# State update ahead of the state read, and the first chunk in order of arrival, in an mLSTM cell followed by a GELU MLP

## The chip, the core and the metric

The kernel runs on one core of a Trainium2 chip. The metric is the time of one execution in microseconds of the device. The engines have short names in all that follows: PE is TensorE (PEld is its weight load), DVE is VectorE, ACT is ScalarE, POOL is GpSimd, and SP is SyncE, which here only issues transfers. Names with a q behind them (ACTq, SPq) are an engine's own queue, where transfers are issued.

## What is computed

The first half is a recurrence over 768 steps for 4 batches of 8 heads of 40 values, and the second half is an MLP of the exact GELU over its output, seen as 3072 tokens of 320 values. The weights arrive as 64-bit floats.

```
for t in range(S):
    m_new = max(f[t] + m, i[t])
    C = exp(f[t] + m - m_new) * C + exp(i[t] - m_new) * outer(v[t], k[t])
    n = exp(f[t] + m - m_new) * n + exp(i[t] - m_new) * k[t]
    m = m_new
    y[t] = sigmoid(o[t]) * (C @ q[t]) / max(abs(n @ q[t]), 1)
x = y as (4 * 768, 320)
out = gelu(x @ w_in) @ w_out          # w_in 320 x 2048, w_out 2048 x 320
```

## The kernel before

The sequence is cut into 6 chunks of 128 steps. Within a chunk the recurrence becomes an attention: the scores of a batch (`scores`, L281: products of turned keys and queries, tile `ps`) are multiplied by weights `W` that hold the gates, and `values` (L323) sums the values with them. What comes from earlier chunks is a second term: the state of the batch (`state`, one tile per batch) is read by the queries (L303), scaled by `gT` into `far` (L306) and added in `values` (L332). The state is then updated for the next chunk: POOL scales the old one by `dec` (L320), PE makes the chunk's own part from keys and weighted values `vw` (L311), and DVE adds the two (L321). Read and update share one tile of PSUM, `pf`: its first 8 columns of heads are the read, the last 4, named `pc`, are the update.

The gates come first. DVE scans `f_gate` to `bl`, subtracts it from `i_gate` to `a`, and a running maximum of `a` gives `M`, chunk by chunk (L147 to L159). `M` goes out to DRAM (`M_d`, L155 for the first chunk and L161 for the rest, both issued by ACT) and comes back copied to all 128 partitions, one tile `Mb` of 512 KB for each batch of each chunk (`load_M`, L113; the first three are issued by ACT, the rest by SP). POOL masks it (L254) and ACT makes `W` from it by 8 exponentials (L257, `weights_of`). Two further gate tiles, `ew` and `gg`, get an exponential (L166, L167), are turned by PE (L172) and copied to `ewT` and `gT`; `dec` is a product of `gT` (L175).

Of the first chunk's steps `turn` (L271) turns keys and queries of a batch on PE and ACT copies them out as `kT` and `qT` (L279); `output_gate` is the sigmoid of `o_gate` (L262); `values` ends in `hs` (copied by ACT in chunk 0, L334), which DVE and POOL divide and gate to `y` (L338 to L345); `turn_y` (L349) turns `y` on PE, and DVE and ACT copy it to `xT` (L356, L357), which the MLP reads.

The weights come as pairs of 32-bit words, in 10 pieces of `w_in` and 16 of `w_out` (`fetch`, L199; four buffers). `convert(i)` (L210) does on DVE and ACT the first half of piece i (L219 to L226; its `pow` goes through ACT twice, L221 and L222) and the second half of piece i - 1 (L231, L233), and then fetches piece i + 3. Ten pieces of `w_in` feed the up projection: its first four steps need pieces 0 to 4, its last four need pieces 5 to 9.

The order is written out by hand: each engine runs its instructions in the order in which the code emits them. A chunk's `run` (L359) emits the steps of four batches, and between them `fill`: in chunk 0 that is `convert`, in later chunks it is groups of four matmuls of the down projection (`po`, L403) of the chunk before. Then comes the up projection (`pu`, L388, and the GELU on ACT, L391). In chunk 0 the remaining conversions and the loads of the next six batches stand between the up steps (L426 to L433). Every batch's q, k, v and o_gate are four transfers of 160 KB by SP (`load`, L96). A chunk's `weights_of(n)` also asks for `Mb` of batch n + NM, where NM is the number of `Mb` buffers.

Of the kernel before, what the change touches and what calls it, by code (L numbers as in the profile page):

```python
# [9 lines left out]
F32 = mybir.dt.float32  # L10
# [10 lines left out]
def kernel(  # L21
# [32 lines left out]
    NM = 3  # L54
    NB = 4
    WP = 512
    assert S % L == 0 and DFF % (4 * WP) == 0 and DM % R == 0 and DM <= WP and D <= DP and NLD > B == 4
# [36 lines left out]
    M_d = dram.tile([BH, S], F32, name="M_d")  # L94
# [36 lines left out]
    for t in state:  # L131
# [15 lines left out]
    nc.vector.tensor_tensor_scan(out=bl.rearrange("p c l -> p (c l)"), data0=keep.rearrange("p c l -> p (c l)"),  # L147
                                 data1=f_sb.rearrange("p c l -> p (c l)"), initial=0.0, op0=OP.mult, op1=OP.add)
    nc.vector.tensor_tensor(out=a, in0=i_sb, in1=bl, op=OP.subtract)
    for c in range(NCH):  # L150
        nc.vector.tensor_tensor_scan(out=M[:, c], data0=a[:, c], data1=a[:, c], initial=m0[:, c:c + 1],
                                     op0=OP.max, op1=OP.max)
        if c == 0:

            nc.scalar.dma_start(out=M_d[:, 0:L], in_=M[:, 0])  # L155
            for n in range(NM):
                load_M(n, nc.scalar)
        if c + 1 < NCH:
            nc.vector.tensor_tensor(out=m0[:, c + 1:c + 2], in0=bl[:, c, L - 1:L], in1=M[:, c, L - 1:L], op=OP.add)  # L159

    nc.scalar.dma_start(out=M_d[:, L:S], in_=M[:, 1:NCH].rearrange("p c l -> p (c l)"))  # L161
# [3 lines left out]
                            in1=M[:, 1:NCH], op=OP.subtract)  # L165
    nc.scalar.activation(out=ew, in_=ew, func=AF.Exp)  # L166
    nc.scalar.activation(out=gg, in_=gg, func=AF.Exp)  # L167
    for src, dst in ((a, aT), (ew, ewT), (gg, gT)):
        n = dst.shape[1]
        pg = ps_tr.tile([P, n, BH], F32, name="pg", tag="tr")  # L170
        for c in range(n):
            nc.tensor.transpose(pg[:, c, :], src[:, c, :], ident[0:BH, 0:BH])  # L172
        nc.vector.tensor_copy(out=dst, in_=pg)
    pd = ps_tr.tile([P, NCH - 1, BH], F32, name="pd", tag="tr")
# [293 lines left out]
```

## Time and profile before

| | |
|---|---|
| Median of 3 runs | 627.89 us (627.11 to 629.42) |
| The profiled execution | 629.21 us, its span 627.3 us |
| PE busy | 554.4 us (88%) in 3850 matmuls |
| PEld busy | 358.1 us (57%) |
| ACT busy | 230.1 us (37%) in 516 |
| DVE busy | 199.0 us (32%) in 442 |
| POOL busy | 81.3 us (13%) in 130 |
| Granted clock of PE, mean | 0.961 |
| Moved by DMA | 43.62 MB in 136233 packets |

The profiled execution is 1.3 us above the median. Busy shares are averages over stages that differ: PE is busy nearly all the time from the first up projection on, and much less in the first 70 us. So the table says only where to look: at PE's own waits, and at the first chunk.

### The profile page before, as it was taken

The page shows a single profiled execution, that of the slowest core. Times are in us where ns is not written, and L with a number is a line of the kernel's source. Part 1 is how long each engine was busy: PE and PEld are TensorE (multiplying, and loading weights), DVE is VectorE, ACT ScalarE, POOL GpSimd, SP SyncE. Part 2 cuts the span into 40 slices and gives each one's busy share as a digit, 9 for nine tenths or more (in the row PEclk, how much of TensorE's full clock was granted, in tenths as well). Part 3 has the DMA queues.
Part 4 walks back from the last instruction along what each step waited for, and adds up shares of the span by engine and source line. Part 5 has one row for each costly group of instructions (what it writes and reads, how often), then busy time and mean ns, then how long its engine had stood idle before and what let it go on. Part 6 is the DMA issues. An engine that isn't in the chain of part 4 may idle for free.

```text
span 627.3 us, 9450 instructions
## 1 busy us (share of the span) xinstructions
PE 554.4 (88%) x3850; PEld 358.1 (57%) x3850; DVE 199.0 (32%) x442; ACT 230.1 (37%) x516; POOL 81.3 (13%) x130
## 2 busy tenths in 40 slices
PE   0637698778999998899999899999899999999997
PEld 0536354456764466764476664476664477754575
DVE  5457686834630013630013630013630014500000
ACT  0775274683022283022284022284022293122200
POOL 4212300012230011230011230011220001100000
PEclk9967699889999999999999999999999999999999
DMA  9999199735430034530034530035200010000000
GB/s 161 208 211 184 37 161 207 178 104 103 76 64 0 1 112 90 82 64 2 0 108 92 81 67 1 0 101 96 46 22 0 1 44 13 11 11 0 1 21 21
DMA packets 136233, 43.62 MB, mean 70 GB/s; under 512 B 101248, under 2 KB 134048, under 8 KB 136192
## 3 DMA queue, kind: packets, MB, share of 16 engines
q1 hardware_dynamic: 132976, 41.36, 33.3%
q10 hardware_dynamic: 3216, 1.67, 1.0%
q8 instruction: 30, 0.49, 0.4%
q14 instruction: 11, 0.09, 0.1%
HBM read 38.99 MB, written 4.03 MB: 69 GB/s over the span
## 4 chain that ended last, share of the span: by engine, by line
PE 49%; issue 38%; POOL 6%; DMA 3%; SPq 2%; DVE 1%; POOLq 0%; ACTq 0%; ACT 0%; DVEq 0%
PE po L403 25%; PE pu L388 11%; PE ph L329 3%; PE ps L293 3%; POOL state L320 2%; POOL Mb L254 2%; DMA Mb<-M_d 2%; PE pf L303 2%; PE pf L311 2%; PE pt L276 2%; SPq L102 2%; PE px L355 1%; SPq L208 1%; POOL vw L286 1%; DMA M_d<-M 1%
## 5 line engine op out<-in xcount | busy, mean ns | idle before, releaser
L403 PE MATMUL po<-w_out,g 128*128 128x320 f32 x768 | 221.0, 437 | 0.0
L388 PE MATMUL pu<-xT,w_in 64*128 64x512 f32 x960 | 215.5, 604 | 3.2 <-ACT g L391 2.8
L403 PEld LDWEIGHTS po<-w_out,g 128*128 128x128 f32 x768 | 141.2, 191 | 52.6 <-issue 1.2
L388 PEld LDWEIGHTS pu<-xT,w_in 64*128 64x128 f32 x960 | 100.6, 192 | 115.7 <-issue 109.5
L296 DVE TENSOR_TENSOR W<-ps,W 128x512 f32<-128x512 f32 x48 | 30.9, 685 | 259.0 <-PE ps L293 259.0
L391 ACT ACTIVATE g<-pu 128x512 f32<-128x512 f32 x96 | 52.0, 593 | 131.9 <-PE pu L388 131.9
L357 ACT COPY xT<-px 64x384 f32<-64x384 f32 (+1 forms) x48 | 17.9, 420 | 128.3 <-DVE xT L356 128.3
L257 ACT ACTIVATE W<-Mb,aT 128x128 f32<-128x128 f32 x192 | 58.1, 393 | 1.8 <-POOL Mb L254 1.7
L320 POOL TENSOR_TENSOR state<-state,dec 64x164 f32<-64x164 f32 x32 | 14.8, 462 | 286.2 <-PE pf L303 285.0
L311 PE MATMUL pf<-vw,kb 128*64 128x41 f32 x320 | 14.1, 239 | 32.1 <-POOL state L320 19.5
L254 POOL TENSOR_SCALAR_AFFINE_SELECT Mb<-Mb 128x1024 f32<-128x1024 f32 x24 | 27.0, 1145 | 80.2 <-DMA Mb<-M_d 80.0
L406 ACT COPY o_sb<-po 128x320 f32<-128x320 f32 x24 | 10.2, 426 | 61.5 <-PE po L403 40.7
L311 PEld LDWEIGHTS pf<-vw,kb 128*64 128x64 f32 x320 | 12.2, 146 | 35.0 <-POOL state L320 21.7
L338 POOL TENSOR_TENSOR y<-hs,ob 128x320 f32<-128x320 f32 x24 | 19.4, 809 | 97.8 <-DVE hs L332 72.1
L293 PEld LDWEIGHTS ps<-qT,kT 64*128 64x128 f32 x384 | 25.8, 205 | 10.1 <-issue 10.1
L293 PE MATMUL ps<-qT,kT 64*128 64x128 f32 x384 | 30.4, 302 | 0.0
L329 PE MATMUL ph<-vb,W 128*64 128x41 f32 x768 | 28.6, 236 | 0.0
L329 PEld LDWEIGHTS ph<-vb,W 128*64 128x64 f32 x768 | 26.4, 145 | 2.4 <-issue 2.2
L356 DVE COPY xT<-px 64x384 f32<-64x384 f32 (+1 forms) x48 | 21.1, 476 | 17.5 <-PE px L355 16.7
L276 PE MATMUL pt<-ident,kb 128*128 128x128 f32 x96 | 17.2, 308 | 9.3 <-ACT kT L279 9.3
L279 ACT COPY kT<-pt 128x512 f32<-128x512 f32 x24 | 14.0, 584 | 30.8 <-PE pt L276 30.6
L355 PE MATMUL px<-ident,y 128*128 128x128 f32 x120 | 18.4, 287 | 6.8 <-ACT xT L357 6.0
(71 smaller groups left out, 352.9 us busy)
## 6 DMA issues: line engine op xcount, KB each, us to landing
Mb<-M_d SPq DMA_DIRECT2D x21, 512.0 KB, 4.0
bits<-in_moe_w_in_dram SPq DMA_DIRECT2D x20, 256.0 KB, 5.6
bits<-in_moe_w_out_dram SPq DMA_DIRECT2D x16, 320.0 KB, 4.2
qb<-in_q_dram SPq DMA_DIRECT2D x24, 160.0 KB, 4.4
kb<-in_k_dram SPq DMA_DIRECT2D x24, 160.0 KB, 4.8
vb<-in_v_dram SPq DMA_DIRECT2D x24, 160.0 KB, 4.3
ob<-in_o_gate_dram SPq DMA_DIRECT2D x24, 160.0 KB, 3.9
out_dram<-o_sb SPq DMA_DIRECT2D x24, 160.0 KB, 1.8
```

Of the source, the lines that this page charges most:

```text
L254: nc.gpsimd.affine_select(out=M_n, in_=M_n, compare_op=OP.is_ge, fill=1.0e30, base=0, pattern=[[0, H], [1, L]], channel_multiplier=-1)
L257: nc.scalar.activation(out=W[n][:, h, :], in_=M_n[:, h, :], func=AF.Exp, scale=-1.0, bias=aT[:, c, b * H + h:b * H + h + 1])
L276: nc.tensor.transpose(pt[:, p, :], src[n % NLD][:, 2 * p:2 * p + 2, :].rearrange("p h d -> p (h d)"), ident)
L293: nc.tensor.matmul(ps[hip][:, p, :], kT[r, p, :], qT[r, p, :], start=True, stop=True)
L296: nc.vector.tensor_tensor(out=w, in0=ps[hip], in1=w, op=OP.mult)
L311: nc.tensor.matmul(pc[halves[hip], p, :], kb[n % NLD][:, 2 * p + hip, :], vw[:, 2 * p + hip, :], start=True, stop=True)
L320: nc.gpsimd.tensor_tensor(out=st, in0=st, in1=d.to_broadcast([DP, NP, D1]), op=OP.mult)
L329: nc.tensor.matmul(ph[r, h, :], Pm[:, h, r], vb[n % NLD][:, h, :], start=True, stop=True)
L355: nc.tensor.transpose(px[:, k, :], ys[:, (k0 + k) * R:(k0 + k + 2) * R], ident)
L388: nc.tensor.matmul(pu[e], w_in[r, k, f // 2 * P:(f // 2 + 1) * P], xT[r, (k - e) % NK, :], start=(k == 0), stop=(k == NK - 1))
L391: nc.scalar.activation(out=g[:, f + e, :], in_=pu[e], func=AF.Gelu)
L403: nc.tensor.matmul(po, g[:, f, b * L:(b + 1) * L], w_out[:, f, :], start=(f == 0), stop=(f == NF - 1))
```

## The change

It has three parts, and each keeps what is computed.

1. In `scores` the eight pairs of matmuls that make `pc` stand ahead of the state read, not behind it and `far`.
2. The first chunk has an order of its own, `run_first`. The first chunk's part of `bl`, `a` and `M` is made ahead of the other five chunks' part. All four `Mb` tiles of chunk 0 are issued by ACT at once (NM is 4). The rest of `M` goes out through SP's queue, behind the first four pieces, and no longer through ACT's. The turning of `a` is followed by `turn(0)`, and that of `ew` and `gg` comes behind it (`decays`). Each batch then goes through `turn`, `scores`, `turn_y` of the batch before, `output_gate`, `values` and one `convert`.
3. `M_d` is stored by chunk, so that a batch's row of `Mb` is one line of 4 KB and not eight of 512 bytes; a transfer of a `w_in` piece has 64 lines of 4 KB and not 256 of 1 KB. `w_in` then holds other columns side by side, and the up step pairs blocks f and f + 4.

```diff
-    NM = 3
+    NM = 4
...
-    M_d = dram.tile([BH, S], F32, name="M_d")
+    M_d = dram.tile([NCH, BH, L], F32, name="M_d")
...
-        eng.dma_start(out=Mb[n], in_=M_d[b * H:(b + 1) * H, c * L:(c + 1) * L]
-                      .unsqueeze(0).to_broadcast([P, H, L]))
+        eng.dma_start(out=Mb[n].rearrange("p h l -> p (h l)"),
+                      in_=M_d[c, b * H:(b + 1) * H, :].rearrange("h l -> (h l)").unsqueeze(0).to_broadcast([P, H * L]))
...
+    for c0, c1 in ((0, 1), (1, NCH)):
+        flat = lambda t: t[:, c0:c1].rearrange("p c l -> p (c l)")
+        nc.vector.tensor_tensor_scan(out=flat(bl), data0=flat(keep), data1=flat(f_sb), initial=0.0,
+                                     op0=OP.mult, op1=OP.add)
+        nc.vector.tensor_tensor(out=a[:, c0:c1], in0=i_sb[:, c0:c1], in1=bl[:, c0:c1], op=OP.subtract)
+        for c in range(c0, c1):
+            nc.vector.tensor_tensor_scan(out=M[:, c], data0=a[:, c], data1=a[:, c], initial=m0[:, c:c + 1],
+                                         op0=OP.max, op1=OP.max)
...
+        if c0 == 0:
+            nc.scalar.dma_start(out=M_d[0], in_=M[:, 0])
+            for n in range(B):
                 load_M(n, nc.scalar)
...
-    nc.scalar.dma_start(out=M_d[:, L:S], in_=M[:, 1:NCH].rearrange("p c l -> p (c l)"))
...
-            src = src.rearrange("k (m two x) -> k m two x", two=2, x=2 * P)
-            pieces.append(([(slice(R * e, R * e + R), src[:, :, e, :]) for e in range(2)],
-                           w_in[:, blk, f0 // 2:f0 // 2 + WP]))
+            pieces.append(([src[:, 2 * WP * e:2 * WP * (e + 1)] for e in range(2)], w_in[:, blk, f0 // 2:f0 // 2 + WP]))
...
+    fetch(0)
+    load(1)
+    fetch(1)
+    load(2)
+    fetch(2)
+    load(3)
+    fetch(3)
+    nc.sync.dma_start(out=M_d[1:NCH].rearrange("c p l -> p c l"), in_=M[:, 1:NCH])
...
             pc = pf[:, H:H + NP, :]
+            if c + 1 < NCH:
+                for p in range(NP):
+                    for hip in range(2):
+                        nc.tensor.matmul(pc[halves[hip], p, :], kb[n % NLD][:, 2 * p + hip, :], vw[:, 2 * p + hip, :],
+                                         start=True, stop=True)
             if c > 0:
...
             if c + 1 < NCH:
-                for p in range(NP):
-                    for hip in range(2):
-                        nc.tensor.matmul(pc[halves[hip], p, :], kb[n % NLD][:, 2 * p + hip, :], vw[:, 2 * p + hip, :],
-                                         start=True, stop=True)
...
+        def run_first(self):
+            self.turn(0), weights_of(0), convert(0)
+            decays()
+            self.scores(0), weights_of(1), convert(1)
+            self.turn(1), weights_of(2), weights_of(3), output_gate(0), self.values(0), convert(2)
+            self.scores(1), self.turn_y(0), output_gate(1), self.values(1), convert(3)
+            self.turn(2), self.scores(2), self.turn_y(1), output_gate(2), self.values(2), convert(4)
+            self.turn(3), self.scores(3), self.turn_y(2), output_gate(3), self.values(3), convert(5)
+            self.turn_y(3)
...
-    conv = feeder([lambda i=i: convert(i) for i in range(len(pieces) + 1)])
-    first = feeder([lambda: conv(1)] * (n_in // 2 + 1))
-    Cell(0).run(first)
+    Cell(0).run_first()
+    conv = feeder([lambda i=i: convert(i) for i in range(n_in // 2 + 1, len(pieces) + 1)])
```

Two places of the order are needed below. The first is PE in the first batch of chunk 1, between the down projection's matmuls; `ps` are the scores, `pf` from `state` is the state read, `pf` from `vw` is the update. Before:

```order
L403 MATMUL po<-w_out,g 128x320 [waits DVE_49] x4
L293 MATMUL ps<-qT,kT 128x128 x8
L303 MATMUL pf<-state_97,qT 64x82 x8
L311 MATMUL pf<-vw,kb_111 64x41 [waits DVE_49,Pool_49]
L311 MATMUL pf<-vw,kb_111 64x41 x7
L403 MATMUL po<-w_out,g 128x320 x4
```

With the change:

```order
L424 MATMUL po<-w_out,g 128x320 [waits DVE_49] x4
L301 MATMUL ps<-qT,kT 128x128 x8
L311 MATMUL pf<-vw,kb_111 64x41 [waits Pool_49]
L311 MATMUL pf<-vw,kb_111 64x41 x7
L316 MATMUL pf<-state_97,qT 64x82 x8
L424 MATMUL po<-w_out,g 128x320 [waits DVE_49] x4
```

The update went ahead of the read and lost its wait for DVE; the read behind it waits for nothing. Its wait for POOL stands for `vw`.

The second place is ACT in chunk 0, from the `hs` of one batch to the `hs` of the next. Before:

```order
L334 COPY hs<-ph 128x328
L221 ACTIVATE pow<-pow,e_hi 128x512
L222 ACTIVATE pow<-pow,e_lo 128x512
L279 COPY kT<-pt 128x512
L279 COPY qT<-pt 128x512
L317 COPY state_99<-pf 64x4x41 x2
L334 COPY hs<-ph 128x328
```

With the change:

```order
L343 COPY hs<-ph 128x328
L225 ACTIVATE pow<-pow,e_hi 128x512
L226 ACTIVATE pow<-pow,e_lo 128x512
L287 COPY kT<-pt 128x512
L287 COPY qT<-pt 128x512
L326 COPY state_99<-pf 64x4x41 x2
L366 COPY xT<-px 64x3x128
L366 COPY xT<-px 64x2x128
L270 ACTIVATE ob_121<-ob_121 128x320
L343 COPY hs<-ph 128x328
```

Before, `hs` of a batch stood behind the turning of the batch two further on, and only one conversion stood in that stretch of the chunk. With the change, `hs` of a batch stands behind a conversion, its own batch's turning, and the copies of the batch before.

## Rows read from the trace of the kernel before

**Rows 1.** The waits of PE: line, for whom, us in total, times, longest

```profile
PE pf L311 <- POOL state L320: 19.5, 16, 1.2
PE pf L311 <- POOL vw L286: 12.6, 2, 10.5
```

**Rows 2.** The timeline in chunk 1, second batch: start, us, engine, line, [idle before <-releaser]

```profile
141.69 1.16 PE L293 MATMUL ps<-qT,kT 64*128 64x128 f32 x16
142.78 0.79 PE L303 MATMUL pf<-state,qT 128*64 128x82 f32 x16
142.95 1.29 DVE L296 TENSOR_TENSOR W<-ps,W 128x512 f32<-128x512 f32 x2 [5.79 <-PE ps L293]
143.66 1.00 POOL L320 TENSOR_TENSOR state<-state,dec 64x164 f32<-64x164 f32 x2 [5.80 <-PE pf L303]
144.16 0.49 DVE L306 TENSOR_TENSOR far<-pf,gT 128x328 f32<-128x328 f32 x1
144.79 0.67 PE L311 MATMUL pf<-vw,kb 128*64 128x41 f32 x16 [1.22 <-POOL state L320]
145.25 1.14 PE L329 MATMUL ph<-vb,W 128*64 128x41 f32 x32
```

**Rows 3.** The timeline of the first 26 us: gates, M and the first weights

```profile
3.06 1.75 DVE L147 TENSOR_TENSOR_SCAN bl<-keep,f_sb 32x768 f32<-32x768 f32 x1 [1.22 <-DMA f_sb<-in_f_gate_dram]
...
5.82 0.47 DVE L151 TENSOR_TENSOR_SCAN M<-a,m 32x128 f32<-32x128 f32 x1
...
11.02 2.98 ACTq L113 DMA_DIRECT2D Mb<-M_d  x3
...
16.15 1.28 ACT L166 ACT_TABLE_LOAD   x1 [16.15 <-DMA Mb<-M_d]
...
16.36 1.09 POOL L254 TENSOR_SCALAR_AFFINE_SELECT Mb<-Mb 128x1024 f32<-128x1024 f32 x1 [9.36 <-DMA Mb<-M_d]
...
18.09 0.72 ACT L167 ACTIVATE gg<-gg 32x640 f32<-32x640 f32 x1
...
23.20 2.45 ACT L257 ACTIVATE W<-Mb,aT 128x128 f32<-128x128 f32 x8
```

**Rows 4.** The timeline from the first `hs` of chunk 0 to the first up matmul

```profile
46.13 1.55 ACT L262 ACTIVATE ob<-ob 128x320 f32<-128x320 f32 x4
...
49.56 0.43 ACT L334 COPY hs<-ph 128x328 f32<-128x328 f32 x1
...
52.11 1.56 PE L329 MATMUL ph<-vb,W 128*64 128x41 f32 x32
...
52.51 0.72 ACT L221 ACTIVATE pow<-pow,e_hi 128x512 f32<-128x512 uint32 x1 [2.52 <-DVE pow L219]
...
54.36 0.59 ACT L279 COPY qT<-pt 128x512 f32<-128x512 f32 x1
...
54.79 1.28 DVE L296 TENSOR_TENSOR W<-ps,W 128x512 f32<-128x512 f32 x2
...
55.77 2.08 PE L293 MATMUL ps<-qT,kT 64*128 64x128 f32 x16
...
58.01 0.87 DVE L356 COPY xT<-px 64x384 f32<-64x384 f32 x2
...
58.58 0.75 ACT L357 COPY xT<-px 64x384 f32<-64x384 f32 x2 [2.69 <-DVE xT L356]
...
70.14 1.99 PE L388 MATMUL pu<-xT,w_in 64*128 64x512 f32 x2 [0.22 <-DVE xT L356]
```

**Rows 5.** Windows: stretch, its us, busy of PE, PEld, DVE, ACT, POOL, PEclk, DMA, GB/s

```profile
50.00:58.00 8.00, 5.53 (x73) 4.83 (x75) 7.49 (x17) 3.31 (x7) 3.05 (x4) 0.66 0.94 200
62.70:72.00 9.30, 3.96 (x14) 2.61 (x16) 6.95 (x15) 3.79 (x8) 4.89 (x5) 0.69 0.02 4
```

**Rows 6.** The line that issues `Mb` (L113), first 40 us, six transfers

```profile
DMA to landing us min/median/max: 5.3/7.3/11.4
```

**Rows 7.** The timeline where chunk 1 starts, PE

```profile
127.90 1.11 PE L276 MATMUL pt<-ident,kb 128*128 128x128 f32 x4 [6.97 <-ACT kT L279]
```

More of the change, by code (lines that the diff above doesn't have):

```diff
@@ L146 @@
     nc.vector.memset(m0[:, 0:1], -1.0e30)
[L147 to L156, printed above, removed]
+    for c0, c1 in ((0, 1), (1, NCH)):
[7 more added lines that the diff above has]
+            if c + 1 < NCH:
+                nc.vector.tensor_tensor(out=m0[:, c + 1:c + 2], in0=bl[:, c, L - 1:L], in1=M[:, c, L - 1:L],
+                                        op=OP.add)
+        if c0 == 0:
+            nc.scalar.dma_start(out=M_d[0], in_=M[:, 0])
+            for n in range(B):
                 load_M(n, nc.scalar)
[L158 to L161 removed]
     nc.vector.tensor_tensor(out=ew, in0=a[:, 0:NCH - 1],
@@ L165, with gates_turned, decays @@
                             in1=M[:, 1:NCH], op=OP.subtract)
+    def gates_turned(parts):
+        for src, dst in parts:
+            n = dst.shape[1]
+            pg = ps_tr.tile([P, n, BH], F32, name="pg", tag="tr")
+            for c in range(n):
+                nc.tensor.transpose(pg[:, c, :], src[:, c, :], ident[0:BH, 0:BH])
+            nc.vector.tensor_copy(out=dst, in_=pg)
+    gates_turned([(a, aT)])
     nc.scalar.activation(out=ew, in_=ew, func=AF.Exp)
     nc.scalar.activation(out=gg, in_=gg, func=AF.Exp)
[L168 to L174, printed above, removed]
-    nc.tensor.matmul(pd.rearrange("p c n -> p (c n)"), last, gT.rearrange("p c n -> p (c n)"), start=True, stop=True)
-    nc.vector.tensor_copy(out=dec, in_=pd)
-    gate_ctx.close()
-    gp = ctx.enter_context(tc.tile_pool(name="gp", bufs=1))
+    def decays():
+        gates_turned([(ew, ewT), (gg, gT)])
+        pd = ps_tr.tile([P, NCH - 1, BH], F32, name="pd", tag="tr")
+        nc.tensor.matmul(pd.rearrange("p c n -> p (c n)"), last, gT.rearrange("p c n -> p (c n)"),
+                         start=True, stop=True)
+        nc.vector.tensor_copy(out=dec, in_=pd)
     w_src = {}
@@ L201, in fetch @@
             return
-        parts, dst = pieces[i]
+        src, dst = pieces[i]
         bits[i] = raw.tile([P, WP, 2], U32, name="bits", tag="bits", bufs=NB)[:, 0:dst.shape[1], :]
-        for r, src in parts:
-            to = bits[i][r].rearrange("p n two -> p (n two)")
-            if len(src.shape) == 3:
-                to = to.rearrange("p (m x) -> p m x", x=2 * P)
-            nc.sync.dma_start(out=to, in_=src)
+        to = bits[i].rearrange("p n two -> p (n two)")
+        for e in range(len(src)):
+            nc.sync.dma_start(out=to[P // len(src) * e:P // len(src) * (e + 1)], in_=src[e])
     def convert(i):
@@ L235, in convert @@
             fetch(i + NB)
-    for n in range(B):
-        if n > 0:
-            load(n)
-        fetch(n)
+    fetch(0)
[6 more added lines that the diff above has]
+    nc.sync.dma_start(out=M_d[1:NCH].rearrange("c p l -> p c l"), in_=M[:, 1:NCH])
     halves = (slice(0, R), slice(R, P))
@@ L380, in up_steps, with step @@
     def up_steps(g):
-        def step(f):
+        def step(i):
+            f = i // (WP // P) * 2 * (WP // P) + i % (WP // P)
             pu = [ps_mm.tile([P, TG], F32, name="pu", tag="mm") for e in range(2)]
-            for k in range(NK):
+            for blk in range(NK):
                 for e in range(2):
                     r = halves[e]
-                    nc.tensor.matmul(pu[e], w_in[r, k, f // 2 * P:(f // 2 + 1) * P], xT[r, (k - e) % NK, :],
-                                     start=(k == 0), stop=(k == NK - 1))
+                    nc.tensor.matmul(pu[e], w_in[r, blk, i * P:(i + 1) * P], xT[r, (blk - e) % NK, :],
+                                     start=(blk == 0), stop=(blk == NK - 1))
             for e in range(2):
-                nc.scalar.activation(out=g[:, f + e, :], in_=pu[e], func=AF.Gelu)
-        return [lambda f=f: step(f) for f in range(0, NF, 2)]
+                nc.scalar.activation(out=g[:, f + e * (WP // P), :], in_=pu[e], func=AF.Gelu)
+        return [lambda i=i: step(i) for i in range(NF // 2)]
     def down_steps(c, g):
```

8 lines of the change are left out of this document (6 added, 2 removed).

## The prediction

> **What bounds the kernel now.** I read the waits of PE first, since PE is busy nearly throughout after the first 70 us. Two of them matter for this change. PE waits 16 times for 1.2 us ahead of the state update, 19.5 us in all [rows 1]: once for each of 4 batches in each of chunks 1 to 4 (chunk 0 has no state to read, chunk 5 none to update). And in chunk 0 it waits for `vw`, 10.5 us the longest time [rows 1]. Next I read the timeline of one of the 16 waits [rows 2]. The state read ends about 143.57. PE then stands until 144.79. In that time POOL scales the old state (143.66 to 144.66), and DVE, which is busy with the weights until 144.24, makes `far` (144.16 to 144.65). The view puts the wait down to POOL, which ended last; the built order names DVE as well. Nothing else of PE's is held there: the update needs only `vw` and keys, and the matmuls behind it, `ph`, start as soon as it is through. Every stage after 133 us is of this kind, PE's own work in a row with this one hole, so 1.22 us saved there is 1.22 us of the end.
>
> Last I read the timeline of chunk 0, which ends with the first up matmul at 70.14 [rows 4]. Here no engine is full. DMA is, until about 60 us (0.94 busy in 50 to 58, and 0.02 in 62.7 to 72 [rows 5]); then a chain over ACT, DVE, POOL and PE runs out, batch by batch.
>
> **Part 1, the update ahead of the read.** No instruction is added or removed: 16 matmuls of 0.67 us and 16 of 0.79 change places [rows 2]. The update then waits for `vw` alone. PE's waits for `vw` are two in the whole run, and the long one lies in chunk 0 [rows 1], so in chunks 1 to 4 `vw` is early even for a place 2 us further ahead (0.8 us of read and 1.2 of wait). The read waits for nothing, as its state was finished a chunk ago. So the hole closes: 16 x 1.22 = **19.5 us**. What comes later instead: POOL's scaling and `far` start when the read ends, now 0.67 us later against the scores but 1.2 us or so earlier against the end; DVE has its weights until then anyway (142.95 to 144.24 [rows 2]). The state is next read a chunk later. Nothing waits for `hs` sooner than the turning of `y`, which stands behind the next batch's scores. I take 19.5 and see no reason for less; the hole in weight loads is a little longer than that in matmuls, which I leave out.
>
> **Part 2, the first chunk.** I walk along the new order with durations of the old one.
>
> Start. From the gates' arrival at 3.06 to M at 5.82 stand `bl` and `a` over 768 columns, 2.76 us [rows 3]. Over 128 columns they cost between a sixth (0.5) and two scans at M's price (2 x 0.47): M starts near 3.85, 2.0 us earlier, and is written out at 4.3. Before, 4.7 us pass from the end of M's scan (6.29) to the issue of `Mb` (11.02) [rows 3]; so `Mb` goes out at 9.0. Three issues held ACT for 2.98 us [rows 3]; four at that rate, 4.0, let ACT go at 13.0, against 16.15 before. M's other five chunks, whose issue held ACT after them, are now SP's.
>
> One rule of the Trainium skill would change this start: the page "DMA: Bandwidth & Descriptors", section "Anatomy of one DMA", puts a transfer's fixed cost near 2.0 us, nearly all of it the receipt of the write. By it ACT would start 2.7 us sooner and the whole sum, as an estimate from that page, be about 605; the trace shows 4.7 for this same write, and I keep the trace.
>
> ACT to the end of the first `hs`, where it has always work and its inputs are there: table load to `gg` 2.66 (16.15 to 18.81 [rows 3]); the first `kT`, `qT` and `pow` 2.44 (52.51 to 54.95 [rows 4]); `W` 2.45 [rows 3]; two copies of the state at the price of two to `xT`, 0.75 [rows 4]; `W` 2.45; `pow`, `kT`, `qT` 2.44; two `W` 4.90; a table load 1.28; one gate of four 0.39; `hs` 0.43 [rows 3, 4]. That is 20.2, so 33.2. Before, this `hs` ended at 49.99 [rows 4]: **17 us later**. For it the first `Mb` has to land by 15.6, 6.6 us after its issue, and be masked in 1.1 [rows 3]; six of them took 5.3 to 11.4 us, 7.3 at the median [rows 6].
>
> Then the order takes most of that back. From `hs` of batch 0 to `hs` of batch 1 DVE is the path: the division, one conversion and the weights, which stand in the same row before (49.99 to 56.07, 6.1), then `ph` 1.56 and `hs` 0.43 [rows 4]: 8.1. From batch 1 to 2, and 2 to 3, ACT is: division, `pow`, `kT`, `qT` (49.99 to 54.95, 4.96); only then the scores (2.08), the weights (1.28), the copies to `xT` (58.01 to 59.33, 1.32), a gate 0.39, `hs` 0.43 [rows 4]: 10.5 each. Before, the turning of the next batches stood ahead of these, and batches followed each other faster. From the last `hs`: division and conversion (49.99 to 54.79, 4.8), `xT` 1.32: 6.1. Sum: 33.2 + 8.1 + 20.9 + 6.1 = 68.3. Some 25 handovers lie between, at 0.05 each as from the read's end to POOL's and DVE's next [rows 2]; with 1.2 for them the first up matmul starts at 69.5, against 70.14. **Gain 0.6 us.**
>
> Bounds of this walk. ACT's start: quicker issues would let it go sooner, but not sooner than the first `Mb` lands, at best 5.3 us after its issue [rows 6] and so 1.3 us less; one issue more that holds as long as all three did is 3.0 us more. The scores and `ph` at the prices that the steady stage shows, 1.16 and 1.14 [rows 2], take off 0.9, 0.9 and 0.4. I take the prices of chunk 0, where the granted clock was 0.66 [rows 5]. So the first up matmul starts between 66.0 and 72.5, a gain of 4.1 or a loss of 2.4.
>
> What the transfers do. The rest of M, now in SP's queue, is waited for by the next `Mb` there, and behind that stands piece 4. Say it goes out at 34, when the fourth piece did before, and lands as late as the slowest `Mb`, 11.4 us [rows 6]: at 45.4. With 5 to 7 us for piece 4 it is there by 52.4; DVE reaches its conversion after the third `hs`, near 54. So it costs nothing; were that cover gone, each us would be one. The long lines make weights and `Mb` arrive no later; I count nothing for them, since behind the first `Mb` the walk waits for no transfer. Load 4 follows piece 8, now fetched near 67, and so goes out some 12 us later than before; the stretch in which DMA stood idle (0.02 [rows 5]) takes it up.
>
> After it. The conversions of the other 21 pieces stand in the same order as before behind the first up matmul, and PE waits 6.97 us for ACT at the start of chunk 1 because ACT still has them [rows 7]. So the shift of the first up matmul goes through to the end one to one. The columns of `w_in` and the pairing of f change no instruction's size.
>
> **Sum.** 629.2 of the profiled execution less 19.5 and 0.6 is 609.1; the median of the runs is 1.3 lower: **607.8**. With the bounds 604 to 611.
>
> **The rivals.**
> - *The first chunk closes up as before.* If batches follow the first `hs` at the old pace (49.99 to 70.14, 20.15 us [rows 4]), the first up matmul is at 33.2 + 20.15 = 53.4, 16.8 us sooner, and the time is 627.9 - 19.5 - 16.8 = 591.6; half way, 600. For it: the first `hs` is early and no transfer is late. Against it: the new order puts `pow`, `kT`, `qT` and the scores one behind the other for each batch, and in-order engines can't step past that.
> - *The first `Mb` come late.* Four of them share DMA with SP's loads, and ACT's first `W` is on the path. At the slowest landing, 11.4 us [rows 6], the first is there at 20.4, 4.8 us later than the walk needs it: 612.6, and up to 618 if the second holds ACT again by as much.
> - *Slower than before.* ACT issues the four `Mb` itself and can't work meanwhile. If each issue holds it until that `Mb` has landed, at the median of 7.3 [rows 6], ACT is free at 9.0 + 29.2 = 38.2, 25.2 us later than in the walk: 633. It decides where the hold takes back the 20.1 and 3.1 beyond, from 6.8 us for each. Against it: three issues took 2.98 together [rows 3], while their landings took 5.3 or more.
> - *The change doesn't do what it says.* The hole could stay if PE waited for POOL's scaling as such. In the new order that scaling stands behind the read, and PE's next matmuls name no wait for it; the time would be 627.3.
>
> **How the numbers follow.** A measurement of this kernel can tell about 0.5% from no change, 3.1 us. Forecast (603 to 612) 0.64; the shorter first chunk (590 to 603) 0.18; late `Mb` (612 to 618) 0.13; the hole stays 0.02; slower 0.03. The range for 8 in 10 takes half of the shorter case and half of the late one: 597 to 614. Faster by over 0.5%: 0.95, within it 0.02, slower 0.03.
>
> **What would show it.** In the profile of the changed kernel PE's wait ahead of the update is gone from the waits, and scores, update and read follow each other without a gap in chunks 1 to 4; a wait of 0.5 us or more at the read or at `ph` would show part 1 wrong. The first `hs` ends near 33 and the first up matmul starts near 69.5, with 8 and twice 10.5 us between the `hs`; a start before 65 or after 73 shows part 2 wrong, and the step in which the walk leaves the trace is the failed one. PE's wait for ACT at the start of chunk 1 stays near 7 us, and the first up matmul stands as far from it as before.

## The result and the profile after

The changed kernel takes **607.07 us** (median of 4 runs, 604.27 to 607.95), the kernel before, measured beside it, 628.5 us (627.11 to 629.42). The ratio is 0.9653, with a 95% interval of 0.9616 to 0.969. The forecast was 607.8, in a range of 597 to 614. The profiled execution took 606.96 us, its span is 605.2 us, 22.1 less than before. The number was right by some luck: two of its terms were off by 2 to 4 us, in opposite directions.

First the waits of PE (line, for whom: us in total, times, longest). These answer to [rows 1]:

```profile
PE ps L301 <- ACT qT L287: 11.8, 3, 4.9
PE pf L311 <- POOL vw L294: 6.3, 1, 6.3
PE pt L284 <- ACT kT L287: 5.4, 1, 5.4
PE pu L409 <- DVE xT L365: 3.6, 1, 3.6
```

The 16 waits of 1.2 us are gone, and so is any wait at the read. In chunk 0 the wait for `vw` became shorter, and a wait for `qT` is new. The timeline of the second batch of chunk 1 (start, us, engine, line) answers to [rows 2]:

```profile
141.20 1.16 PE L301 MATMUL ps<-qT,kT 64*128 64x128 f32 x16
...
142.29 0.67 PE L311 MATMUL pf<-vw,kb 128*64 128x41 f32 x16
142.46 1.29 DVE L304 TENSOR_TENSOR W<-ps,W 128x512 f32<-128x512 f32 x2 [5.12 <-PE ps L301]
...
142.78 0.77 PE L316 MATMUL pf<-state,qT 128*64 128x82 f32 x16
...
143.38 1.08 PE L338 MATMUL ph<-vb,W 128*64 128x41 f32 x32
...
143.66 0.49 DVE L319 TENSOR_TENSOR far<-pf,gT 128x328 f32<-128x328 f32 x1
...
144.39 4.58 PE L424 MATMUL po<-w_out,g 128*128 128x320 f32 x16
```

Before, the down matmuls behind `ph` began here:

```profile
146.32 4.04 PE L403 MATMUL po<-w_out,g 128*128 128x320 f32 x14
```

From the start of the scores to the start of these down matmuls it was 146.32 - 141.69 = 4.63 us before [rows 2], and it is 144.39 - 141.20 = 3.19 now. A batch saves **1.44 us**, not the 1.22 of the wait. Matmul groups overlap at their edges: the group behind the read began 2.01 us after the read's start before, and begins 0.60 after it now, though the read itself takes 0.77. The idle time that the view of waits counts leaves out the overlap that the hole also takes away. (The profile models the ends of matmuls; the 1.44 is a distance between starts.)

To see where the rest went, the program is cut at the first turning of keys of each chunk. Before (timeline of PE, chunks 1, 2 and 5):

```profile
115.52 0.66 PE L276 MATMUL pt<-ident,kb 128*128 128x128 f32 x4
...
218.73 0.66 PE L276 MATMUL pt<-ident,kb 128*128 128x128 f32 x4
...
502.17 0.66 PE L276 MATMUL pt<-ident,kb 128*128 128x128 f32 x4
```

After:

```profile
117.25 0.66 PE L284 MATMUL pt<-ident,kb 128*128 128x128 f32 x4
...
213.91 0.66 PE L284 MATMUL pt<-ident,kb 128*128 128x128 f32 x4
...
480.12 0.66 PE L284 MATMUL pt<-ident,kb 128*128 128x128 f32 x4
```

| Stretch | Before, us | After, us | Difference |
|---|---|---|---|
| start to the first up matmul | 70.14 | 72.14 | +2.00 |
| first up matmul to chunk 1's first turning | 45.38 | 45.11 | -0.27 |
| chunk 1 | 103.21 | 96.66 | -6.55 |
| chunks 2 to 4 | 283.44 | 266.21 | -17.23 |
| from chunk 5's first turning to the end | 125.13 | 125.08 | -0.05 |

Chunks 2 to 4 save 5.74 us each, 4 x 1.44. So part 1 brings 16 x 1.44 = **23.0 us**. The first chunk takes back 2.0. Of the remaining 1.1, 0.8 lies at chunk 1's start: PE waits 5.41 us for `kT` where it waited 6.97 [rows 7], and the eight down matmuls behind it then take 3.78 us in place of 3.02. Behind that wait PE's granted clock is 0.50, its lower level of 1.2 GHz, until 132, and 0.62 in the next us; before, it was 0.50 until 131 and 0.97 in the next. Over the 6.6 us from that wait's end it is 0.65, where it was 0.76.

Chunk 0, with ACT's issues, its two waits, and its four `hs` (timeline of ACT, then DVE's wait for a piece of `w_in`, then PE's first up matmul):

```profile
7.49 2.54 ACTq L113 DMA_DIRECT2D Mb<-M_d  x4
...
15.90 2.45 ACT L265 ACTIVATE W<-Mb,aT 128x128 f32<-128x128 f32 x8 [2.23 <-POOL Mb L262]
...
24.06 0.72 ACT L225 ACTIVATE pow<-pow,e_hi 128x512 f32<-128x512 uint32 x1 [1.40 <-DVE pow L223]
...
32.99 0.41 ACT L343 COPY hs<-ph 128x328 f32<-128x328 f32 x1
...
41.30 0.43 ACT L343 COPY hs<-ph 128x328 f32<-128x328 f32 x1
...
52.55 0.43 ACT L343 COPY hs<-ph 128x328 f32<-128x328 f32 x1
...
64.31 0.43 ACT L343 COPY hs<-ph 128x328 f32<-128x328 f32 x1 [0.54 <-PE ph L338]
```

```profile
23.59 0.43 DVE L223 TENSOR_SCALAR pow<-bits 128x512 uint32<-128x512 uint32 x1 [4.22 <-DMA bits<-in_moe_w_in_dram]
...
72.14 3.78 PE L409 MATMUL pu<-xT,w_in 64*128 64x512 f32 x7 [3.60 <-DVE xT L365]
```

The first `hs` ends at 33.40, where 33.2 was forecast; the steps to the next ones are 8.33, 11.25 and 11.76 us (forecast 8.1, 10.5, 10.5), and from the last to the first up matmul 7.40 (6.1, and 1.2 of handovers in all).

### The profile page after: what moved, and what is told of

Read it like the earlier page. It is cut to its first block, busy times and chain, and to the rows that moved or that the text cites. A ratio compares the mean times of both kernels' runs of the same rounds, so it can differ in the third digit from the quotient of the medians.

```text
span 605.2 us, 9445 instructions
## 1 busy us (share of the span) xinstructions
PE 555.8 (92%) x3850; PEld 359.6 (59%) x3850; DVE 199.3 (33%) x444; ACT 230.6 (38%) x516; POOL 79.9 (13%) x130
## 4 chain that ended last, share of the span: by engine, by line
PE 81%; DVE 7%; DMA 6%; ACT 3%; issue 1%; SPq 1%; DVEq 0%; ACTq 0%
PE po L424 35%; PE pu L409 30%; PE ps L301 4%; PE ph L338 4%; PE pt L284 3%; DMA bits<-in_moe_w_out_dram 3%; PE px L364 2%; PE pf L316 2%; PE pf L311 2%; DVE sig L230 1%; DVE pow L235 1%; DMA Mb<-M_d 1%; DVE pow L223 1%; DMA kb<-in_k_dram 1%; DVE sig L228 1%
## 5 line engine op out<-in xcount | busy, mean ns | idle before, releaser
L225 ACT ACTIVATE pow<-pow,e_hi 128x320 f32<-128x320 uint32 (+1 forms) x26 | 16.2, 623 | 28.0 <-DVE pow L223 28.0
L287 ACT COPY kT<-pt 128x512 f32<-128x512 f32 x24 | 14.0, 582 | 22.0 <-PE pt L284 21.8
L284 PE MATMUL pt<-ident,kb 128*128 128x128 f32 x96 | 16.8, 303 | 6.1 <-ACT kT L287 5.4
L364 PE MATMUL px<-ident,y 128*128 128x128 f32 x120 | 19.5, 299 | 3.0 <-DVE y L353 3.0
```

The costliest lines, as they stand in the source:

```text
L284: nc.tensor.transpose(pt[:, p, :], src[n % NLD][:, 2 * p:2 * p + 2, :].rearrange("p h d -> p (h d)"), ident)
L364: nc.tensor.transpose(px[:, k, :], ys[:, (k0 + k) * R:(k0 + k + 2) * R], ident)
```

## The experiments

Each kernel was timed beside the kernel before on the same chip; that one's medians were 628.0 to 629.0 us.

**1. Part 1 alone.** In the kernel before:

```diff
             pc = pf[:, H:H + NP, :]
+            if c + 1 < NCH:
+                for p in range(NP):
+                    for hip in range(2):
+                        nc.tensor.matmul(pc[halves[hip], p, :], kb[n % NLD][:, 2 * p + hip, :], vw[:, 2 * p + hip, :],
+                                         start=True, stop=True)
             if c > 0:
...
             if c + 1 < NCH:
-                for p in range(NP):
-                    for hip in range(2):
-                        nc.tensor.matmul(pc[halves[hip], p, :], kb[n % NLD][:, 2 * p + hip, :], vw[:, 2 * p + hip, :],
-                                         start=True, stop=True)
```

> The kernel before with part 1 alone (the update ahead of the state read). First theory, from the trace after the change: a batch of chunks 1 to 4 loses 1.44 us from the start of its scores to the next down matmul (4.63 before, 3.19 after), so 16 x 1.44 = 23.0 us in all; the time is 605 and chunk 2 starts are 88.7 us apart in place of 94.5. Rival, the prediction: 16 x 1.22 = 19.5, time 608.4, starts 89.6 apart. Either way the first up matmul stays at 70.1, and PE's wait for kT where chunk 1 starts stays near 7.0.

Measured: 605.88 us against 628.83, ratio 0.9644 (0.9616 to 0.9672): 22.95 us, the first theory. The 16 waits are gone from its view of waits; chunks 3 to 5 start at 302.08, 390.81 and 479.55, 88.74 apart. The first up matmul is at 70.92, the wait for `kT` is 7.06.

**2. All but part 1.** The changed kernel, with the edit of experiment 1 reversed: the update stands behind the read again.

```diff
-            if c + 1 < NCH:
-                for p in range(NP):
...
             if c + 1 < NCH:
+                for p in range(NP):
```

> The changed kernel with part 1 undone (read, far, update again). If the parts add up, the wait of 1.22 us is back 16 times, chunk starts are 94.5 apart, and the time is 607.1 + 23.0 = 630, so parts 2 and 3 together cost 1 to 2 us against the 628 of before: the first up matmul is at 72.1, 2.0 later than before. Rival: parts 2 and 3 bring something elsewhere that the trace hides, and the time is under 626.

Measured: 628.43 us against 628.83, ratio 1.0001 (0.9986 to 1.0017). The 16 waits are back, 19.5 us in all, and the chunks are 94.48 apart. The first up matmul is at 71.19 and not at 72.1: the start of the same chunk 0 differs by a us from one execution to another. Parts 2 and 3 together bring nothing that can be measured. The first `hs` ends at 33.2 here and at 50.0 before, so a gain of 17 us is given back within the chunk. The expected 630 was 1.6 too much: it took that one execution's 2.0 us for the cost of the parts.

**3. Part 3 alone.** In the kernel before:

```diff
-    M_d = dram.tile([BH, S], F32, name="M_d")
+    M_d = dram.tile([NCH, BH, L], F32, name="M_d")
...
-            src = src.rearrange("k (m two x) -> k m two x", two=2, x=2 * P)
-            pieces.append(([(slice(R * e, R * e + R), src[:, :, e, :]) for e in range(2)],
+            pieces.append(([(slice(R * e, R * e + R), src[:, 2 * WP * e:2 * WP * (e + 1)]) for e in range(2)],
...
+            f = i // (WP // P) * 2 * (WP // P) + i % (WP // P)
```

> The kernel before with part 3 alone (M_d by chunk, pieces of w_in in lines of 4 KB, up steps pairing f and f + 4; NM stays 3). First theory: behind the first Mb chunk 0 waits for no transfer, so the first up matmul stays within 1 us of 70.1 and the time within 1 us of 628. Rival: the short lines set the pace of chunk 0 (DMA 0.94 busy until 60 us), the first up matmul comes 3 us or more sooner and the time is 625 or less.

Measured: 628.19 us against 628.83, ratio 0.9998 (0.9973 to 1.0022); first up matmul at 71.32. No difference, but not for the reason expected: in the old order DVE does wait for transfers, for four pieces of `w_in`. Before, then with long lines (waits of DVE):

```profile
DVE pow L219 <- DMA bits<-in_moe_w_in_dram: 9.3, 4, 3.3
DVE pow L218 <- DMA bits<-in_moe_w_in_dram: 13.5, 4, 4.0
```

Long lines let ACT go 2.8 us sooner, at 13.31 in place of 16.12. But the four conversions that wait start within 0.5 us of where they started before, so what ACT wins ends in longer waits of DVE.

**4. The changed order with short lines.** The changed kernel with part 3 undone, which is the edit of experiment 3 reversed:

```diff
-    M_d = dram.tile([NCH, BH, L], F32, name="M_d")
+    M_d = dram.tile([BH, S], F32, name="M_d")
...
-            pieces.append(([src[:, 2 * WP * e:2 * WP * (e + 1)] for e in range(2)], w_in[:, blk, f0 // 2:f0 // 2 + WP]))
+            src = src.rearrange("k (m two x) -> k m two x", two=2, x=2 * P)
+            pieces.append(([(slice(R * e, R * e + R), src[:, :, e, :]) for e in range(2)],
```

> The changed kernel with part 3 undone (short lines for Mb and the pieces of w_in). First theory, from the pipelined order with short lines: ACT issues the four Mb itself, and with short lines it is held until about 16 in place of 10.0; the waits of 2.2 and 1.4 us that ACT has before its first hs take up part of it, so the first hs comes 2 to 6 us later, the first up matmul at 74 to 78, and the time is 609 to 613: part 3 pays in this order for what part 2 costs. Rival: the order of the changed kernel hides it, the first up matmul stays within 1 us of 72.1 and the time within 1.5 us of 607.

Measured: 608.65 us against 627.95, ratio 0.9681 (0.9663 to 0.9698). ACT's four issues (timeline of ACT):

```profile
8.43 6.14 ACTq L113 DMA_DIRECT2D Mb<-M_d  x4
```

They hold ACT until 14.57, 4.5 us later than with long lines (10.03): 3.6 by their length and 0.9 by a later start, which long lines show too in another execution (8.69 in experiment 2). The first `hs` ends at 35.77, 2.4 later, and the first up matmul starts at 74.33, 2.2 later. The trace shows the first theory at its lower end, and the time lies just under it. It is 1.6 us above the changed kernel's, with overlapping intervals, so on the time alone it would be open.

**5. POOL held.** In the changed kernel, behind the last `turn_y` of chunk 0:

```diff
             self.turn_y(3)
+            nc.gpsimd.tensor_copy(out=hold, in_=xT[0:1, NK - 1, TG - 1:TG])
```

> The changed kernel with one element copied on POOL behind the last xT of chunk 0, so that POOL's three masks of chunk 1's Mb (3.71 us) no longer run beside the last batch's division and conversion. First theory: those masks stretch DVE's work there (the product with den 1.02 for 0.67, the copy of y 0.97 for 0.20, the first step of sig 1.31 for 0.42: 2.0 us), so the first up matmul comes at 70.1 in place of 72.1, and the time is 605. Rival: the masks then stretch the conversions behind the first up matmul by as much, chunk 1 starts as late as before, and the time stays 607.

Measured: 604.54 us, ratio 0.9619 (0.959 to 0.9647), so 2.5 us less than the changed kernel, with overlapping intervals; the trace tells more. The end of chunk 0 in the changed kernel (timeline of POOL and DVE):

```profile
65.58 3.71 POOL L262 TENSOR_SCALAR_AFFINE_SELECT Mb<-Mb 128x1024 f32<-128x1024 f32 x3
...
66.00 1.02 DVE L353 TENSOR_TENSOR y<-y,den 128x320 f32<-128x320 f32 x1
67.05 0.97 DVE L354 COPY y<-y 128x64 f32<-128x64 f32 x1
...
68.27 1.31 DVE L228 TENSOR_SCALAR sig<-bits 128x512 uint32<-128x512 uint32 x1
```

And with POOL held, to the first up matmul and just behind it:

```profile
65.89 0.49 DVE L354 TENSOR_TENSOR y<-y,den 128x320 f32<-128x320 f32 x1
66.42 0.20 DVE L355 COPY y<-y 128x64 f32<-128x64 f32 x1
...
69.85 6.57 PE L411 MATMUL pu<-xT,w_in 64*128 64x512 f32 x21 [2.03 <-DVE xT L366]
...
70.19 0.31 POOL L379 COPY hold<-xT 1x1 f32<-1x1 f32 x1 [4.67 <-DVE xT L366]
70.39 3.53 DVE L229 TENSOR_SCALAR sig<-bits 128x512 uint32<-128x512 uint32 x1
...
70.46 3.17 POOL L263 TENSOR_SCALAR_AFFINE_SELECT Mb<-Mb 128x1024 f32<-128x1024 f32 x3
```

The same three DVE instructions take 0.49, 0.20 and 0.42 without the masks beside them. From the end of the last `hs` to the first up matmul it is 5.21 us in place of 7.40, and that matmul comes 2.29 us sooner. One conversion step, begun beside the copy that holds POOL, then lasts 3.53 us in place of 0.42, until behind the last mask. That costs nothing here: in the changed kernel DVE waits 5.5 us for ACT's `pow` in that stretch, and with POOL held only 1.0.

**6. The turning ahead.** In `run_first` of the changed kernel:

```diff
-            self.turn(1), weights_of(2), weights_of(3), output_gate(0), self.values(0), convert(2)
-            self.scores(1), self.turn_y(0), output_gate(1), self.values(1), convert(3)
-            self.turn(2), self.scores(2), self.turn_y(1), output_gate(2), self.values(2), convert(4)
-            self.turn(3), self.scores(3), self.turn_y(2), output_gate(3), self.values(3), convert(5)
+            self.turn(1), weights_of(2), weights_of(3), output_gate(0), self.turn(2), self.values(0), convert(2)
+            self.scores(1), self.turn_y(0), output_gate(1), self.turn(3), self.values(1), convert(3)
+            self.scores(2), self.turn_y(1), output_gate(2), self.values(2), convert(4)
+            self.scores(3), self.turn_y(2), output_gate(3), self.values(3), convert(5)
```

> The changed kernel with the turning of batches 2 and 3 moved ahead of the values of batches 0 and 1; everything else stays. First theory: in the changed kernel batches 2 and 3 have their conversion (pow on ACT), their turning and their scores one behind the other, which makes their hs come 11.3 and 11.8 us apart. With the turning out of that row the path is DVE's as from batch 0 to 1, 8.3 us each, the first hs is 1.1 later, and the first up matmul comes near 66 to 67 in place of 72.1; the time is 601 to 602. Rival: the pieces of w_in or the rest of M arrive too late for the faster pace, the first up matmul stays at 70 or later, and the time within 2 us of 607.

Measured: 603.68 us, ratio 0.9605 (0.958 to 0.9629; it overlaps that of the changed kernel a little), first up matmul at 69.28. Batches 2 and 3 now follow at 8.4 and 8.3 us, as expected. But batch 1 follows batch 0 at 11.4, because the turning of batch 3 now stands on PE between `turn_y(0)` and the values of batch 1, and there waits 3.1 us for ACT to copy `xT` (both use the two buffers of PSUM for turned tiles). Half the gain was paid at another place.

**7. Another order for chunk 0.** `run_first` becomes:

```diff
+            self.turn(0), convert(0), weights_of(0, False)
+            decays()
+            weights_of(1, False), self.scores(0), self.turn(1), weights_of(2, False), convert(1)
+            nc.sync.dma_start(out=M_d[1:NCH].rearrange("c p l -> p c l"), in_=M[:, 1:NCH])
+            self.scores(1), self.turn(2), weights_of(3, False)
+            for b in range(2):
+                output_gate(b)
+            self.values(0), self.scores(2), self.values(1), self.turn_y(0), self.turn(3), convert(2)
+            load_M(4), load_M(5)
+            self.turn_y(1), self.scores(3), output_gate(2), self.values(2), convert(3)
+            load_M(6), load_M(7)
+            output_gate(3), self.values(3), self.turn_y(2), convert(4), self.turn_y(3), convert(5)
```

where `False` leaves out `weights_of`'s own `load_M`.

> The changed kernel with another order in chunk 0: conversion 0 ahead of the first W, scores of batches 0 and 1 and the turning of batch 2 ahead of the first values, then values of one batch beside the scores of one further on, the last conversion behind the last turning of y; the rest of M and the Mb of chunk 1 are issued behind piece 4. First theory: order alone sets the pace of chunk 0. The first hs comes at 32 to 33 as now, DVE then has 22 to 25 us of work in a row, and the first up matmul starts near 57, 15 us sooner; the time is about 592. Rival: transfers set it (pieces 3 and 4 land after 45), DVE waits for bits, the first up matmul starts at 65 or later and the time is 600 or more. Second rival: the conversions behind the first up matmul can't start sooner, PE's wait for kT where chunk 1 starts grows by what was won, and the time stays near 605.

Measured: 596.14 us, ratio 0.9479 (0.9458 to 0.9499). The second and the last `hs` and the first up matmul:

```profile
36.11 0.43 ACT L343 COPY hs<-ph 128x328 f32<-128x328 f32 x1 [1.11 <-PE ph L338]
...
51.15 0.41 ACT L343 COPY hs<-ph 128x328 f32<-128x328 f32 x1
```

```profile
59.14 5.49 PE L413 MATMUL pu<-xT,w_in 64*128 64x512 f32 x11 [1.68 <-DVE xT L365]
```

The first up matmul comes 13.0 us sooner, and 10.9 of that reach the end; the wait for `kT` at chunk 1 grows from 5.4 to 7.0. The first theory holds, with a size that was 2 us (chunk 0) and 4 us (time) too good. So it was for the most part the order that gave the 17 us back: 13.0 come back with another one. This edit also moves the issue of the rest of `M` and of chunk 1's `Mb`; but in the changed kernel no engine waits for a transfer between the first `hs` and the first up matmul.

**8. The same, with POOL held** as in experiment 5:

```diff
             output_gate(3), self.values(3), self.turn_y(2), convert(4), self.turn_y(3), convert(5)
+            nc.gpsimd.tensor_copy(out=hold, in_=xT[0:1, NK - 1, TG - 1:TG])
```

> The order of the run before this one, and POOL held by one element copied behind the last xT, so that its masks of chunk 1 don't run beside DVE's last steps of chunk 0. If the masks cost there what they cost in the changed kernel (2.3 us at the first up matmul, 2.5 in the time), the first up matmul is near 55 and the time about 590. Rival: with the last conversion moved behind, DVE has less there that the masks stretch, and the gain is under 1 us.

Measured: 598.19 us, ratio 0.9511 (0.9493 to 0.9529), 2 us more than without. The first up matmul is where it was (59.20), but chunk 0 ran 1.4 us late in this execution: its last `hs` ends at 52.99 in place of 51.56. From there to the first up matmul it is 6.21 us in place of 7.58, so the hold does win 1.4 us, between the two theories. Two conversion steps behind it are stretched (2.48 and 1.58 us in place of 0.42 and 0.69). DVE itself makes that up: in experiment 7 it waited 2.1 us for ACT's `pow` in that stretch, here not at all, and by 74.1 it is 0.3 us behind. But the stretched steps free a buffer of pieces 2.5 us later (64.43 in place of 61.97), SP fetches what comes next about as much later, and DVE waits for it. The waits for pieces of `w_in` in experiment 7, then here (waits of DVE):

```profile
DVE pow L223 <- DMA bits<-in_moe_w_in_dram: 3.3, 2, 3.0
DVE pow L224 <- DMA bits<-in_moe_w_in_dram: 5.3, 2, 3.1
```

The second of the two was 0.25 and is 2.21 us, and PE's wait for `kT` ends at 119.45 in place of 117.64. Neither theory had the 2 us.

**9. The order of 7 with short lines**, by the edit of experiment 4.

> The pipelined order of chunk 0 (xT as in the changed kernel) with part 3 undone: M_d by sequence, Mb in lines of 512 bytes, pieces in lines of 1 KB, up steps of f and f + 1. First theory: transfers are still no bound, DVE reaches the pieces late enough; the first up matmul stays within 1 us of 59.1 and the time within 1.5 us of 596. Rival: with the shorter chain transfers have lost their cover, the first Mb or pieces 2 to 4 come late, the first up matmul is 2 us or more later and the time is 598 or more: then part 3 is worth something only where the order lets it.

Measured: 600.19 us, ratio 0.9547 (0.9518 to 0.9576), 4.0 more than with long lines, first up matmul at 64.31, 5.2 later. ACT's issues, with long lines (experiment 7) and with short ones:

```profile
8.01 2.24 ACTq L113 DMA_DIRECT2D Mb<-M_d  x4
```

```profile
9.11 6.88 ACTq L113 DMA_DIRECT2D Mb<-M_d  x4
```

The rival holds, but not at the place it named. What came later is ACT itself: it is free at 15.99 in place of 10.25, 5.7 us (4.6 by the length of the issues, 1.1 by their later start), and its first `hs` ends 5.96 us later. The pieces are not what came late: DVE waits 1.40 us for one here, and 3.02 in experiment 7. Part 3 works through the issues, and is worth more the less slack ACT has behind them: nothing in the old order, 2.2 us at the first up matmul in the changed one, 5.2 here.

**10. `xT` by ACT.** In the order of 7, ACT copies both halves of `xT` in chunk 0:

```diff
-                nc.vector.tensor_copy(out=xT[0:R, k0:k0 + n, t], in_=px[0:R])
+                (nc.scalar.copy if self.c == 0 else nc.vector.tensor_copy)(out=xT[0:R, k0:k0 + n, t], in_=px[0:R])
```

> The pipelined order of chunk 0, and both halves of xT copied by ACT in chunk 0. First theory: DVE is the bound there (from the first hs at 31.7 to the first up matmul at 59.1 it stands 4.1 us), ACT is not; four copies of 0.87 off DVE, 3.5 us, bring the first up matmul to 55.7 and the time to 593. Rival: the copies then come one behind the other on ACT, ahead of pow and hs, and the first up matmul comes no sooner than 58.5; the time stays at 596.

Measured: 594.24 us, ratio 0.9454 (0.9429 to 0.9479), first up matmul at 57.40: 1.7 us sooner of the 3.5 that DVE lost in work. Counted from the first `hs`, which ended 1.1 us later in this execution (32.69 in place of 31.63), it is 2.8. The time is 1.9 us less than in experiment 7, with overlapping intervals, where the first theory had 3; this is the fastest order found, with the next one.

**11. Gates early.** As 10, and:

```diff
-            self.scores(1), self.turn(2), weights_of(3, False)
+            self.scores(1), self.turn(2)
             for b in range(2):
                 output_gate(b)
-            self.values(0), self.scores(2), self.values(1), self.turn_y(0), self.turn(3), convert(2)
+            self.values(0), weights_of(3, False), self.scores(2), self.values(1), self.turn_y(0), self.turn(3), convert(2)
```

> The same, and the first two output gates and the first values ahead of the weights of batch 3, at the price of two more table loads of 1.28 on ACT. First theory: the first hs comes 2.45 us sooner, DVE fills its wait of 5.1 us with the first division, and the first up matmul comes 1 to 2 us sooner than in the run before this one. Rival: the two loads and the later W of batch 3 hold ACT by as much; no difference.

Measured: 594.14 us, ratio 0.9455 (0.9429 to 0.9481), first up matmul at 57.00. The rival: no difference, though the first `hs` came 2.3 us sooner.

**12. Whom the update waited for.** In the kernel before, POOL scales each half of the state twice:

```diff
                         nc.gpsimd.tensor_tensor(out=st, in0=st, in1=d.to_broadcast([DP, NP, D1]), op=OP.mult)
+                        nc.gpsimd.tensor_tensor(out=idle[r], in0=st, in1=d.to_broadcast([DP, NP, D1]), op=OP.mult)
```

> The kernel before with POOL's scaling of the state done twice (the second result goes to a tile that nobody reads), so POOL is busy 2.0 us where it was 1.0. If PE's update waits for POOL, as the view of the waits names it, the hole of 1.22 us grows to 2.2 and the time by up to 16 us. If it waits for DVE's far, as the built order has it, the hole stays 1.2 and the time within 2 us of 628.

Measured: 624.45 us, a single run; the hole is unchanged. The view of waits, then the rows of DVE, POOL and PE in one such hole:

```profile
PE pf L312 <- POOL idle L322: 19.5, 16, 1.2
```

```profile
139.80 0.49 DVE L307 TENSOR_TENSOR far<-pf,gT 128x328 f32<-128x328 f32 x1
139.84 0.46 POOL L322 TENSOR_TENSOR idle<-state,dec 64x164 f32<-64x164 f32 x1
140.38 0.46 POOL L321 TENSOR_TENSOR state<-state,dec 64x164 f32<-64x164 f32 x1
140.44 0.67 PE L312 MATMUL pf<-vw,kb 128*64 128x41 f32 x16 [1.22 <-POOL idle L322]
...
140.92 0.47 POOL L322 TENSOR_TENSOR idle<-state,dec 64x164 f32<-64x164 f32 x1
```

PE starts while POOL's scaling still runs (140.38 to 140.84), and 0.15 us after the end of `far` (140.29). The wait was DVE's. The view named whatever of POOL's happened to end at that moment, now a result that nobody reads. The time itself is 4.3 us below the other runs of before, more than the 2 expected, and all of it lies ahead of that place: PE's wait for `kT` where chunk 1 starts ends at 123.05 in place of 127.90 [rows 7], and from there to the end it is 499.5 us, where it was 499.4. What made these first stages shorter is open; the scaling has no part in them, as chunk 0 has none.

## Why the prediction came out right

The forecast span was 627.3 - 19.5 - 0.6 = 607.2; measured were 605.2, 2.0 less. That is 3.5 less by part 1, 2.6 more by chunk 0, and 1.1 less between the first up matmul and the end, most of it at chunk 1's start. The first up matmul of the same chunk 0 differs by a us between two executions (experiment 2), so the last two are rough.

- **Part 1: the mechanism right, the size 3.5 too small.** The hole closed and nothing took its place. The step that failed is to price the hole by its idle time, and in it "the hole in weight loads is a little longer than that in matmuls, which I leave out": that one was 1.36 us, which makes 21.8. The price is not the idle time but the distance between the starts of the groups around the hole: 1.44 and not 1.22, 16 times. Experiment 1 shows the 23.0 alone.
- **Part 2, the start: two errors that met.** `Mb` went out at 7.49 and not at 9.0, as the write of `M` took 3.2 us until then and not 4.7, and the four issues took 2.54 and not 4.0: ACT was free at 10.03, 3 us sooner than in the walk. But "it has always work and its inputs are there" was wrong: ACT waited 2.23 us for the first masked `Mb` and 1.40 for the conversion whose piece DVE was waiting for. That the first `hs` ended within 0.2 us of the forecast was luck.
- The Trainium skill's page "DMA: Bandwidth & Descriptors", section "Anatomy of one DMA", by which the estimate was 605, gives its 2.0 us for transfers that POOL's queue issues; this write is ACT's. The trace does not agree with 2.0 for it: the write landed 3.1 us after its issue here, and 3.1 to 4.9 in the 14 traces. And ACT's sooner start did not go through to the first `hs`, as that sum needs: its two waits took it back.
- **Part 2, the batches: right in kind, 2.4 us too short from the first `hs` on** (38.74 us, forecast 36.3 with the handovers). The row of scores, weights and copies to `xT` left out what PE has to do in between. In batch 2 of the changed kernel:

```profile
46.74 2.08 PE L301 MATMUL ps<-qT,kT 64*128 64x128 f32 x16 [3.58 <-ACT qT L287]
...
48.75 1.08 PE L311 MATMUL pf<-vw,kb 128*64 128x41 f32 x16
...
49.76 1.27 PE L364 MATMUL px<-ident,y 128*128 128x128 f32 x5
...
50.70 0.88 DVE L365 COPY xT<-px 64x384 f32<-64x384 f32 x2 [0.56 <-PE px L364]
...
51.28 0.75 ACT L366 COPY xT<-px 64x384 f32<-64x384 f32 x2 [0.81 <-DVE xT L365]
```

  The turning of `y` waits its turn behind the update on PE, so DVE stands 0.56 us behind the weights. In batch 3 `ph` takes 1.94 in place of 1.13, and ACT stands 0.54 more. The tail was priced with the first batch's division (4.8 us), which has no masks beside it. The last one has, in the kernel before too, so the price was there to be read; experiment 5 puts 2.2 us on it. The handovers, 1.2 in the forecast, are in these steps.
- **Transfers: right for the rest of `M` and piece 4, wrong for one piece and for the issues.** The rest of `M` went out at 33.35 (34 in the forecast) and landed in 4.8; piece 4 was never waited for. But "behind the first `Mb` the walk waits for no transfer" did not hold: DVE waited 4.22 us for the piece of its second conversion, and ACT 1.40 behind it. And the long lines, for which the forecast counts nothing, set how long four issues hold ACT: 2.54 or 6.14 (experiment 4).
- **After the first up matmul: one to one**, as forecast, to within some us. To chunk 1's first turning it is 45.38 and 45.11 us. To the end of the wait for `kT` it is 57.76 and 55.93, and 54.7 to 57.8 in the other runs with these two orders. PE's wait for `kT` fell by 1.56, since DVE waited 0.43 and not 1.98 us for the last piece; the forecast had it unchanged.
- **The rivals.** That the hole stays is refuted by experiments 1 and 2. "The first chunk closes up as before" was wrong for this order, and experiments 7 and 10 show that another order gets most of it (13.0 and 14.7 us of 16.8 at the first up matmul). The slower rival, ACT held by its own issues, is a real mechanism: 6.14 and 6.88 us with short lines, far from its 29. Late `Mb` did not come true: the first was there at 14.77, when POOL began to mask it, and the walk needed it at 15.6. ACT waited 2.23 us for it because it was itself 3 us early.

## What to carry to other kernels

Where in-order engines hand work to each other, a matmul that needs nothing new belongs ahead of one whose result somebody must read; price such a hole by the distance between the starts of the groups around it, not by the wait alone. An early start of a chain is worth only what its slowest queue lets through: here a first result 17 us sooner changed nothing that could be measured (experiment 2). When conversions, turnings and values were reordered for all engines together, the time fell by 10.9 us (596.1 in place of 607.1), and with `xT` copied by ACT by 12.8. Before pricing an instruction, look at what runs beside the row that it was taken from.

## What the runs showed of the hardware

POOL and DVE stop each other. Beside the end of chunk 0, three DVE steps of 0.49, 0.20 and 0.42 us took 1.02, 0.97 and 1.31, and POOL's three masks 3.71 in place of 3.17 (the changed kernel and experiment 5). And a DVE step of 0.42 us took 3.53: it began at 70.39, within POOL's copy of one element (70.19 to 70.50), and ended 0.29 us after the three masks behind that. The Trainium skill's page "SBUF — State Buffer", section "SBUF: two separate sides", says of the port pair that POOL shares with some kinds of DVE operation that whichever starts first has it for the whole instruction and "the other fully blocks". The trace agrees in that POOL had started first and DVE's 0.42 us became 3.53; that the block here lasted over four instructions of POOL, and in the changed kernel over one at a time, the page does not say.

Four transfers of 512 KB that ACT issues held it 2.24 to 2.76 us in lines of 4 KB and 6.14 and 6.88 us in lines of 512 bytes, though the engine only issues them (the lines of the pieces that SP issues meanwhile changed with them, 4 KB and 1 KB). The write of the 16 KB of `M` to adjoining lines in DRAM landed 3.1 to 4.9 us after its issue, and to lines 3 KB apart 3.8 to 4.8: the layout makes no difference that these traces could show.
